# Two token blocks share each half of the first feed-forward's weights; partial sums of x1 go through DRAM

## Chip, core and metric

The kernel runs on one core of a Trainium2 chip. The metric is device time in microseconds, median over runs; lower is better. The engines are TensorE (PE; its weight loads are PEld), VectorE (DVE), ScalarE (ACT), GpSimd (POOL) and SyncE (SP, which here only issues DMAs). Each works through its own list of instructions in order, and waits where a semaphore isn't there yet.

## The reference

Chunked attention, and then two feed-forwards over its 3072 tokens of width 512. What matters of it:

```python
# attention per 32-query chunk c: keys and values = 8 memory rows + window of 56 around the chunk
scores = scale * np.matmul(q_c, k_full.transpose(0, 1, 3, 2))
a = np.exp(scores - np.max(scores, axis=-1, keepdims=True))
a = a / (np.sum(a, axis=-1, keepdims=True) + 1e-09)
out[:, :, c_start:c_end] = np.matmul(a, v_full)
...
h = x @ w_in                                              # 512 -> 2048
g = np.where(h > 0.0, h, np.exp(np.minimum(h, 0.0)) - 1)  # ELU
x1 = g @ w_out                                            # 2048 -> 512
...
y = ((x1 @ w1) * (x1 @ w2)) @ w3 @ w_out2
```

The inputs of the feed-forwards are 64-bit floats in DRAM.

## The kernel before

The tokens are cut into NB = 8 blocks of TB = 384, and a block into GPB = 3 attention groups of 128 queries (24 groups G in all). Every product is made of three passes in a 32-bit format (`mm3`, L125 to L128): each operand is split in a high part (cast on ACT) and a low part (subtraction on DVE).

**First feed-forward.** FF1 = 16 tiles of 128 columns. Iteration n = 16j + f works on block j and tile f. Below, H(n) is `mm_h` (12 matmuls into one of two PSUM banks), E(n) the ELU (`elu_exp`: two ACT steps; `elu_split`: L472 on DVE, a cast on ACT, L123 on DVE) and X(n) is `mm_x` (12 matmuls that add to PSUM banks 0 to 3). PE has them in the order H(n), X(n-2), H(n+1), X(n-1), and so on. After a block's last X, `store_x1` copies banks 0 to 3 out (two copies on ACT, two on DVE) and stores them in DRAM (`x1d`). At such a boundary X stands ahead of H in the first two iterations of the next block.

**The feed.** `Feed` turns the 32 weight tiles of this feed-forward (w_in: slots 0 to 15, w_out: slots 16 to 31) from 64-bit rows into high and low parts. Job i is spread over three steps: `rebase` on ACT (L161) once the raw tile has landed, then `shift` and `low` on DVE (L165, L169), then the cast `hi_of` on ACT (L174) and `lo_of` on DVE (L177). 34 steps finish 32 jobs. A step also loads a raw tile some jobs ahead, 512 KB on SP's queue. The intermediate `f` lies in the pool f_p, four buffers, which the copies of `store_x1` (name `st`) share.

**Attention.** A group goes through `at_turn` (T: transposes of q and k, three copies on ACT), `at_turn2` (U: four small transposes, two copies), `at_scores` (S), `at_max`, `at_sum`, `at_norm`, `at_flip` (DVE, with one exponential on ACT), `at_values` (V) and `at_out` (a cast on ACT, L123 on DVE, into xhl, the input of the first feed-forward). From group 3 on they all use one PSUM pair ("banks") and one buffer of each tile, and the next group's q, k and v are loaded as soon as those are free. Groups 0 to 2 run ahead of the first iteration by the list START, in which "f" is a feed step and "t0 u0 s0 m0 z0 n0 p0 v0 o0" are group 0's parts. The other groups are spread over the iterations by `plan`: parts at steps 0 to 9 from a group's start, two steps in an iteration, 32 steps for three groups. From group 6 on the steps also carry the conversion of the second feed-forward's weights (`mid_jobs`).

**Second feed-forward.** In the last block of the first, freed weight slots are refilled and `load_x1`/`split_x1` bring x1 of block 0 back into xhl; then w3 and w_out2 are multiplied together, and the eight blocks run through `mm_ab` and `mm_o`.

Of the kernel before, what the change touches and what calls it, by code (L numbers as in the profile page):

```python
# [19 lines left out]
def tile_kernel(  # L20
# [41 lines left out]
    AT_BLOCK = 32  # L62
# [5 lines left out]
    LATER = (10, 11, 12, 13, 14, 15, 25, 26, 27, 28, 29, 30, 31)  # L68
# [25 lines left out]
    wabd = [[dram.tile([P, 2, 512], F32, name=f"wabd{c}_{r}") for r in range(2)] for c in range(FF2)]  # L94
    x1d = [dram.tile([P, KT, TB], F32, name=f"x1d{j}") for j in range(NB)]
# [93 lines left out]
    class Feed:  # L189
# [222 lines left out]
    def store_next():  # L412
# [14 lines left out]
    for G in range(GPB, NG):  # L427
        s0 = AT_BLOCK * (G - GPB) // GPB
        for at, fn in plan:
            steps[s0 + at].append((fn, G))  # L430
        if G >= GM:
            n = [(G - GM + i) * n_others // (NG - GM) for i in range(2)]
            for job, at in zip([others.pop(0) for _ in range(n[1] - n[0])], (0, 6)):
                mid_jobs.append(job)
                for i, fn in enumerate((rebase, mid_low, mid_split)):
                    steps[s0 + at + i].append((fn, job))
                if at == 0 and w3s:
                    job = w3s.pop(0)
                    mid_jobs.append(job)
                    for at3, fn in ((4, rebase), (5, mid_low), (9, mid_flip)):  # L440
                        steps[s0 + at3].append((fn, job))
    assert not others and not w3s
    at_done, at_most = [0], [0]

    def at_step():
        if at_done[0] < min(at_most[0], len(steps)):
            store_next()
            for fn, G in steps[at_done[0]]:
                fn(G)
            at_done[0] += 1  # L450
# [3 lines left out]

    def mm_h(n):
        j, f = divmod(n, FF1)
# [19 lines left out]
    def mm_x(n):  # L476
        j, f = divmod(n, FF1)
        g, w = g_t.pop(n), W[FF1 + f]
        for o in range(KT):
            c = slice(o * P, (o + 1) * P)  # L480
            mm3(PS[o][:, 0:TB], w[:, 0, c], w[:, 1, c], g[:, 0, :], g[:, 1, :], f == 0, f == FF1 - 1)

    def store_x1(j):
        for o in range(KT):
            t = f_p.tile([P, 512], F32, tag="f", name="st")
            copy_on("av"[o % 2], t[:, 0:TB], PS[o][:, 0:TB])
            nc.sync.dma_start(out=x1d[j][:, o, :], in_=t[:, 0:TB])
# [69 lines left out]
    with tc.manual_schedule():  # L557
# [12 lines left out]
        def run(what):  # L570
            for ch in what:
                if ch == "f":
                    feed.step()
                else:
                    at_step()
# [30 lines left out]
        for n in range(NH + 2):  # L606
            j, f = divmod(n, FF1)
            while f == 0 and at_done[0] < min(AT_BLOCK * j, len(steps)):
                at_step()
            at_most[0] = AT_BLOCK * (j + 1)  # L610
            first = f < 2 and j > 0
# [6 lines left out]
            if n == FF1:  # L618
# [6 lines left out]
            if n >= 2 and first:  # L625
                mm_x(n - 2)
                if f == 1 and n < NH:
                    store_x1(j - 1)
# [100 lines left out]
```

## Time and profile before

| | |
|---|---|
| median of 3 runs | 1152.84 us (1149.68 to 1154.06) |
| the profiled execution's own time | 1151.45 us |
| its span, first to last instruction | 1149.7 us |
| PE busy | 1095.1 us, 95% of the span, 8800 matmuls |
| DVE busy, ACT busy | 493.9 us (43%), 431.2 us (38%) |
| DMA | 124.78 MB, mean 109 GB/s |

Shares over the whole span hide that the kernel has stages. In the 40 slices of the page PE reads 3, 6 and four times 8 tenths before it comes to 9, and DVE reads 4, 5 and four times 8 in the same slices and 5 and 6 afterwards. So the start and block 0, up to about 145 us, are to be read apart from the rest: there the rows below ask who is busy and who waits, engine by engine, in order of time.

### The profile page before, as it was taken

What the parts mean: (1) busy time and instruction counts of PE and PEld (TensorE: products, weight loads), DVE (VectorE), ACT (ScalarE), POOL (GpSimd) and SP (SyncE); (2) the same over time, 40 slices, a digit from 0 to 9 for tenths busy, and PEclk for the clock granted to TensorE, in tenths of its full rate; (3) what the DMA queues carried; (4) which work ended last, traced back from release to release, by engine and by line L of the source; (5) the groups of instructions that cost most, each with busy time, mean ns of one, the idle gap of its engine ahead of it and who ended that gap; (6) DMA issues with size and microseconds to landing.
All of it is one profiled execution on the core that took longest, in us unless ns stands there. A gap on an engine that the chain in (4) does not pass through costs nothing.

```text
span 1149.7 us, 20882 instructions
## 1 busy us (share of the span) xinstructions
PE 1095.1 (95%) x8800; PEld 1031.9 (90%) x8800; DVE 493.9 (43%) x912; ACT 431.2 (38%) x897; POOL 2.1 (0%) x16
## 2 busy tenths in 40 slices
PE   3688899999999999999999999999999999999998
PEld 2587789989989999999999998799999999999997
DVE  4588855555655565565655331122221212222111
ACT  3366545454544555444544441122221212122111
POOL 0000000000000000000000000000000000000000
PEclk8699999999999999999999999999999999999999
DMA  8855454444554533643630885310000101000000
GB/s 182 230 143 152 123 169 133 146 148 118 153 152 128 167 118 109 175 129 110 180 101 38 271 280 176 112 32 28 28 29 28 55 1 56 29 28 28 1 28 28
DMA packets 153100, 124.78 MB, mean 109 GB/s; under 512 B 103856, under 2 KB 136624, under 8 KB 153008
## 3 DMA queue, kind: packets, MB, share of 16 engines
q1 hardware_dynamic: 151968, 123.20, 36.0%
q8 instruction: 69, 1.13, 0.4%
q10 hardware_dynamic: 1040, 0.26, 0.1%
q14 instruction: 23, 0.19, 0.1%
HBM read 89.88 MB, written 33.55 MB: 107 GB/s over the span
## 4 chain that ended last, share of the span: by engine, by line
PE 83%; DVE 7%; ACT 4%; DMA 3%; issue 1%; SPq 1%; DVEq 0%; ACTq 0%
PE bank L126 22%; PE bank L128 21%; PE bank L127 21%; PE banks L126 4%; PE banks L128 4%; PE banks L127 4%; PE banks L378 2%; DMA x1d<-st 1%; PE banks L319 1%; DVE f L169 1%; DVE w L177 1%; ACT g L122 1%; DMA vw<-in_v_dram 1%; DVE eg L472 1%; PE banks L293 1%
## 5 line engine op out<-in xcount | busy, mean ns | idle before, releaser
L126 PE MATMUL bank<-xhl,w 128*128 128x384 f32 x768 | 266.9, 347 | 11.7 <-DVE eg L472 9.1
L128 PE MATMUL bank<-xhl,w 128*128 128x384 f32 x768 | 260.7, 339 | 0.0
L127 PE MATMUL bank<-xhl,w 128*128 128x384 f32 x768 | 260.3, 339 | 0.0
L122 ACT CAST g<-eg 128x384 fp32r<-128x384 f32 x192 | 98.4, 512 | 297.0 <-DVE eg L472 156.5
L126 PE MATMUL bank<-g,w 128*128 128x384 f32 x512 | 176.8, 345 | 0.0
L128 PE MATMUL bank<-g,w 128*128 128x384 f32 x512 | 172.3, 337 | 0.0
L127 PE MATMUL bank<-g,w 128*128 128x384 f32 x512 | 172.1, 336 | 0.0
L123 DVE TENSOR_TENSOR g<-eg,g 128x384 fp32r<-128x384 f32 x192 | 107.3, 559 | 133.9 <-ACT g L122 133.9
L126 PEld LDWEIGHTS bank<-xhl,w 128*128 128x128 f32 x768 | 146.4, 191 | 20.0 <-DVE eg L472 8.0
L538 DVE TENSOR_TENSOR eg<-eg,banks 128x384 f32<-128x384 f32 x64 | 35.4, 553 | 271.8 <-PE banks L128 271.8
L127 PEld LDWEIGHTS bank<-xhl,w 128*128 128x128 f32 x768 | 146.4, 191 | 3.2 <-DVE xhl L123 0.4
L128 PEld LDWEIGHTS bank<-xhl,w 128*128 128x128 f32 x768 | 146.1, 190 | 0.0
L126 PEld LDWEIGHTS bank<-g,w 128*128 128x128 f32 x512 | 96.5, 188 | 2.3
L127 PEld LDWEIGHTS bank<-g,w 128*128 128x128 f32 x512 | 96.6, 189 | 0.2 <-DVE g L123 0.2
L128 PEld LDWEIGHTS bank<-g,w 128*128 128x128 f32 x512 | 96.5, 188 | 0.0
L537 ACT COPY eg<-bank 128x384 f32<-128x384 f32 x64 | 30.7, 480 | 171.4 <-PE bank L128 171.4
L465 ACT ACTIVATE eg<-bank 128x384 f32<-128x384 f32 x128 | 62.6, 489 | 69.4 <-PE bank L128 69.4
L472 DVE SCALAR_TENSOR_TENSOR eg<-eg,bank 128x384 f32<-128x384 f32 x128 | 69.6, 544 | 41.3 <-ACT eg L466 40.9
L128 PE MATMUL banks<-xhl,w 128*128 128x384 f32 x256 | 85.7, 335 | 0.0
L126 PE MATMUL banks<-xhl,w 128*128 128x384 f32 x256 | 85.6, 335 | 0.0
L127 PE MATMUL banks<-xhl,w 128*128 128x384 f32 x256 | 85.6, 334 | 0.0
L128 PE MATMUL bank<-w,g 128*128 128x512 f32 x192 | 76.0, 396 | 0.0
(99 smaller groups left out, 1290.6 us busy)
## 6 DMA issues: line engine op xcount, KB each, us to landing
raw<-in_moe_w_dram SPq DMA_DIRECT2D x32, 512.0 KB
raw<-in_moe_w_out_dram SPq DMA_DIRECT2D x20, 512.0 KB
w3d<-st SPq DMA_DIRECT2D x16, 512.0 KB
wabd<-st SPq DMA_DIRECT2D x16, 512.0 KB
w<-w3d SPq DMA_DIRECT2D x16, 512.0 KB
w<-wabd SPq DMA_DIRECT2D x16, 512.0 KB
raw<-in_moe_w_in_dram SPq DMA_DIRECT2D x12, 512.0 KB
x1d<-st SPq DMA_DIRECT2D x32, 192.0 KB
```

The costliest lines, as they stand in the source:

```text
L122: nc.scalar.copy(hi, src)
L123: nc.vector.tensor_tensor(out=lo, in0=src, in1=hi.bitcast(F32), op=ALU.subtract)
L126: mm(o, lhsT=w_hi, rhs=x_hi, start=start, stop=False)
L127: mm(o, lhsT=w_hi, rhs=x_lo, start=False, stop=False)
L128: mm(o, lhsT=w_lo, rhs=x_hi, start=False, stop=stop)
L169: nc.vector.scalar_tensor_tensor(out=t, in0=l, scalar=29, in1=t, op0=ALU.logical_shift_right, op1=ALU.bitwise_or)
L177: nc.vector.tensor_tensor(out=job.to[:, 1, :], in0=job.f if src is None else src, in1=job.to[:, 0, :].bitcast(F32), op=ALU.subtract)
L378: mm(o, lhsT=vw[cc, u, 2 * hp + r, :], rhs=pT[cc, r, hp, u, :], start=u == 0, stop=u == 1)
L465: nc.scalar.activation(e, h_t[n], AF.Relu, scale=-1.0)
L472: nc.vector.scalar_tensor_tensor(out=e, in0=e, scalar=-1.0, in1=ph, op0=ALU.add, op1=ALU.max)
L537: nc.scalar.copy(e, pab[0])
L538: nc.vector.tensor_tensor(out=e, in0=e, in1=pab[1], op=ALU.mult)
```

## The change

Blocks 0 and 1 now go through tiles 0 to 7 one after the other, and then both through tiles 8 to 15 (`PARTS`); blocks 2 to 7 stay as they were. `seq` gives the block and tile of iteration n, so n = 0 to 7 is block 0, 8 to 15 block 1, 16 to 23 block 0 again, 24 to 31 block 1 again. At the end of each half the sums are stored: the first halves into `x1p`, the second into `x1d`, so that there are boundaries at n = 8 and n = 24 beside those at 16 and 32. For blocks 0 and 1 `load_x1` loads both, and `split_x1` adds them on DVE (four additions a block). The feed's jobs are in the order of the halves; its two steps an iteration go on up to n = 17, and begin at n = 0 instead of n = 2. Block 1's attention (groups 3 to 5) has to be done by n = 8 and runs at the pace "fast", half as many steps from part to part; block 2's begins at step 38 rather than 32. START has one feed step less, and v0 stands ahead of u2 and s2.

```diff
-    START = "t0 u0 f s0 t1 f m0 u1 s1 z0 n0 m1 p0 f t2 u2 s2 v0 z1 n1 p1 o0 m2 v1 f z2 n2 p2 o1 v2 f o2 f"
-    IN_BLOCK0 = ("fa", "fa", "")
+    START = "t0 u0 f s0 t1 f m0 u1 s1 z0 n0 m1 p0 t2 v0 u2 s2 f z1 n1 p1 o0 m2 v1 f z2 n2 p2 o1 v2 f o2"
+    HALF = FF1 // 2
+    PARTS = [(0, 0, HALF), (1, 0, HALF), (0, HALF, FF1), (1, HALF, FF1)] + [(j, 0, FF1) for j in range(2, NB)]
...
+    x1p = [dram.tile([P, KT, TB], F32, name=f"x1p{j}") for j in range(2)]
...
+    paces = {
+        "slow": (0, 1, 1, 2, 3, 4, 5, 6, 8, 8, 9), "fast": (0, 0.5, 0.5, 1, 1.5, 2, 2.5, 3, 4, 4, 4.5),
+        "mid": (0, 1, 1, 2, 3, 4, 5, 5, 7, 7, 7.5),
+    }
...
+    def base(G):
+        if G < 2 * GPB:
+            return 5 * (G - GPB), "fast"
+        if G < 3 * GPB:
+            return ((38, "slow"), (47, "mid"), (55, "mid"))[G - 2 * GPB]
+        return 4 * FF1 + 2 * FF1 * (G - 3 * GPB) // GPB, "slow"
...
+    seq = [(j, f, f - f0, f == f1 - 1) for j, f0, f1 in PARTS for f in range(f0, f1)]
...
-    def store_x1(j):
+    def store_x1(j, to):
...
+            for src in ((x1d, x1p) if j < 2 else (x1d,)):
+                t = late.tile([P, TB], F32, tag="x1" if src is x1d else "x1p", name="x1", bufs=4)
...
+            if len(ts) > 1:
+                nc.vector.tensor_tensor(out=ts[0], in0=ts[0], in1=ts[1], op=ALU.add)
...
-        order = sorted(range(2 * FF1), key=lambda i: i if i < FF1 else i - FF1 + 2)
+        order = sorted(range(2 * FF1), key=lambda i: (i % FF1 // HALF, i if i < FF1 else i - FF1 + 2))
...
+            def x():
+                if n >= 2:
+                    if n < 3 * FF1 // 2 + 2:
+                        feed.until(due[FF1 + seq[n - 2][1]])
+                    mm_x(n - 2)
+                    if at == 1 and n < NH:
+                        p = n // HALF - 1
+                        store_x1(seq[n - 2][0], x1p if p < 2 else x1d)
+                if n < FF1 + 2:
+                    feed.step()
+                at_step()
```

What the change moves on the engines, at three places. In these listings L291, L293, L305, L319 and L378 of before are L294, L296, L308, L322 and L381 of after, and L117, L161, L174, L465 and L466 are L120, L164, L177, L484 and L485.

PE, ahead of block 0, before: group 2 (its PSUM is pair_101) and the V of groups 0 and 1 (banks, pair_100).

```order
L291 MATMUL pair_101<-ident,qn 128x128 x4
L293 MATMUL pair_101<-ident,kn 128x128 x4
L305 MATMUL pair_101<-ident,kn 128x32 x4
L319 MATMUL pair_101<-kT,qT 32x64 x32
L378 MATMUL banks<-pT,vw 64x64 x32
L378 MATMUL pair_100<-pT,vw 64x64 x32
```

The same place after:

```order
L294 MATMUL pair_101<-ident,qn 128x128 x4
L296 MATMUL pair_101<-ident,kn 128x128 x4
L381 MATMUL banks<-pT,vw 64x64 x32
L308 MATMUL pair_101<-ident,kn 128x32 x4
L322 MATMUL pair_101<-kT,qT 32x64 x32
L381 MATMUL pair_100<-pT,vw 64x64 x32
```

V of group 0 has moved ahead of U and S of group 2.

PE at the first iterations, before, with buffer numbers (w0, w1, w2 are the tiles of H(0), H(1), H(2); w16 that of X(0)) and group 3's parts between them:

```order
L128 MATMUL bank4_95<-xhl0_73,w0_75 128x384
L291 MATMUL banks_94<-ident_72,qn_590 128x128 x4
L293 MATMUL banks_94<-ident_72,kn_166 128x128 x4
L126 MATMUL bank5_96<-xhl0_73,w1_76 128x384
...
L305 MATMUL banks_94<-ident_72,kn_166 128x32 x4
L126 MATMUL bank4_95<-xhl0_73,w2_77 128x384
...
L319 MATMUL banks_94<-kT_640,qT_638 32x64 x32
L126 MATMUL bank0_603<-g_643,w16_85 128x384
```

The same place after:

```order
L131 MATMUL bank4_95<-xhl0_73,w0_75 128x384
L294 MATMUL banks_94<-ident_72,qn_584 128x128 x4
L296 MATMUL banks_94<-ident_72,kn_168 128x128 x4
L308 MATMUL banks_94<-ident_72,kn_168 128x32 x4
L322 MATMUL banks_94<-kT_634,qT_632 32x64 x32
L129 MATMUL bank5_96<-xhl0_73,w1_76 128x384
...
L129 MATMUL bank4_95<-xhl0_73,w2_77 128x384
...
L381 MATMUL banks_94<-pT_736,vw_167 64x64 x32
L129 MATMUL bank0_597<-g_692,w16_84 128x384
```

T, U and S of group 3 now stand together ahead of H(1), and its V ahead of X(0).

ACT at the first boundary of before (n = 17), with the counters that each instruction waits for (DMAHW is a DMA's landing; the others name engines):

```order
L122 CAST g_1699<-eg_1682 128x384 [waits DVE_49]
L117 COPY st_1715<-bank0_603 128x384 [waits PE_49]
L117 COPY st_1721<-bank2_605 128x384 [waits PE_49]
L174 CAST st_1760<-f_1668 128x512
L465 ACTIVATE eg_1775<-bank5_96 128x384 [waits PE_49]
```

ACT at the first boundary of after (n = 9), where x1p of block 0 is stored. DMAHW6 is the landing of the store of st_1357, DMAHW0 that of st_1363, and DMAHW3 a raw tile's:

```order
L125 CAST g_1341<-eg_1330 128x384 [waits DVE_49]
L120 COPY st_1357<-bank0_597 128x384 [waits PE_49]
L120 COPY st_1363<-bank2_599 128x384 [waits DMAHW6_49,PE_49,Activation_49]
L177 CAST w25_93<-f_1314 128x512
L164 ACTIVATE f_1373<-raw_1292 128x512 [waits DMAHW3_49,DMAHW0_49,Activation_49]
L484 ACTIVATE eg_1389<-bank5_96 128x384 [waits PE_49]
```

Two feed jobs hold their `f` here, so the four copies have two buffers between them: the second copy on ACT waits for the first one's store, and the next rebase for the second one's.

## Rows read from the trace of the kernel before

**Rows 1.** Windows: busy time by engine in three stretches, with granted clock.

```profile
core 0: us, PE busy (x) PEld busy (x) DVE busy (x) ACT busy (x) POOL busy (x), PEclk, DMA share, GB/s
28.00:57.00 29.00, 18.69 (x299) 16.41 (x300) 15.67 (x28) 10.96 (x22) 0.00 (x0) 0.59 0.81 234
57.00:86.00 29.00, 25.19 (x251) 23.53 (x249) 25.15 (x47) 18.26 (x39) 0.00 (x0) 0.94 0.52 144
500.00:600.00 100.00, 100.00 (x1053) 96.00 (x1052) 58.20 (x107) 50.01 (x107) 0.00 (x0) 1.00 0.45 132
```

**Rows 2.** Timeline of DVE around two attention groups: start, us, line, [idle before].

```profile
95.68 0.69 DVE L336 TENSOR_REDUCE mx<-banks 128x8 f32<-128x512 f32 x1
...
97.01 0.55 DVE L472 SCALAR_TENSOR_TENSOR eg<-eg,bank 128x384 f32<-128x384 f32 x1
...
100.39 0.68 DVE L344 TENSOR_REDUCE sm<-e 128x8 f32<-128x512 f32 x1
...
101.64 0.42 DVE L165 TENSOR_SCALAR f<-f 128x512 int32<-128x512 int32 x1
...
103.31 1.29 DVE L356 TENSOR_TENSOR e<-e,rc 128x512 f32<-128x512 f32 x2
104.51 0.55 DVE L472 SCALAR_TENSOR_TENSOR eg<-eg,bank 128x384 f32<-128x384 f32 x1
105.64 0.56 DVE L123 TENSOR_TENSOR g<-eg,g 128x384 fp32r<-128x384 f32 x1 [0.58 <-ACT g L122]
106.12 0.42 DVE L165 TENSOR_SCALAR f<-f 128x512 int32<-128x512 int32 x1
...
107.79 1.24 DVE L367 STREAM_TRANSPOSE pT<-e 128x1024 f32<-128x1024 f32 x1
108.95 0.38 DVE L165 TENSOR_SCALAR f<-f 128x512 int32<-128x512 int32 x1
```

**Rows 3.** The same for the last steps of E(1) and E(14).

```profile
58.85 0.56 DVE L123 TENSOR_TENSOR g<-eg,g 128x384 fp32r<-128x384 f32 x1 [0.58 <-ACT g L122]
...
143.20 0.56 DVE L123 TENSOR_TENSOR g<-eg,g 128x384 fp32r<-128x384 f32 x1 [0.58 <-ACT g L122]
```

**Rows 4.** The same for group 0's output and group 2's maximum, ahead of block 0.

```profile
31.76 0.69 DVE L123 TENSOR_TENSOR xhl<-banks,xhl 128x512 fp32r<-128x512 f32 x1 [4.96 <-ACT xhl L122]
...
33.70 0.42 DVE L165 TENSOR_SCALAR f<-f 128x512 int32<-128x512 int32 x1
```

**Rows 5.** Chain of work that ended last: start, us, what; ahead of block 0.

```profile
20.76 4.07 DMA raw<-in_moe_w_in_dram
...
45.37 5.44 DMA kn<-in_k_dram
```

**Rows 6.** Timeline of PE: the first matmul of H(0), T(3), the first of H(1).

```profile
42.54 0.69 PE L126 MATMUL bank<-xhl,w 128*128 128x384 f32 x1 [0.68 <-ACT xhl L122]
...
49.53 1.12 PE L291 MATMUL banks<-ident,qn 128*128 128x128 f32 x4 [2.37 <-DMA qn<-in_q_dram]
...
51.62 0.67 PE L126 MATMUL bank<-xhl,w 128*128 128x384 f32 x1
```

**Rows 7.** Chain again: the stores at the boundaries n = 17 and n = 33.

```profile
154.51 2.76 DMA x1d<-st
...
234.37 4.45 DMA x1d<-st
```

**Rows 8.** Timeline of DVE: the second copy of `store_x1` at n = 17.

```profile
157.39 0.56 DVE L119 COPY st<-bank 128x384 f32<-128x384 f32 x1 [2.23 <-DMA x1d<-st]
```

**Rows 9.** Timeline of PE: S(6), X(16) first and last, the first matmul of H(20).

```profile
153.19 0.86 PE L319 MATMUL banks<-kT,qT 64*32 64x64 f32 x64 [1.56 <-ACT kT L308]
...
158.27 0.33 PE L126 MATMUL bank<-g,w 128*128 128x384 f32 x1
...
160.17 0.34 PE L128 MATMUL bank<-g,w 128*128 128x384 f32 x1
...
165.92 0.45 PE L126 MATMUL bank<-xhl,w 128*128 128x384 f32 x1 [0.86 <-DVE eg L472]
```

More of the change, by code (lines that the diff above doesn't have):

```diff
@@ L427, in tile_kernel @@
     for G in range(GPB, NG):
-        s0 = AT_BLOCK * (G - GPB) // GPB
-        for at, fn in plan:
-            steps[s0 + at].append((fn, G))
+        s0, pace = base(G)
+        for at, fn in zip(paces[pace], chain):
+            put(s0 + at, fn, G)
         if G >= GM:
             n = [(G - GM + i) * n_others // (NG - GM) for i in range(2)]
-            for job, at in zip([others.pop(0) for _ in range(n[1] - n[0])], (0, 6)):
+            for job, at in zip([others.pop(0) for _ in range(n[1] - n[0])], (0, 5)):
                 mid_jobs.append(job)
                 for i, fn in enumerate((rebase, mid_low, mid_split)):
-                    steps[s0 + at + i].append((fn, job))
-                if at == 0 and w3s:
+                    put(s0 + at + i, fn, job)
+                if at == 0 and w3s and pace == "slow":
                     job = w3s.pop(0)
                     mid_jobs.append(job)
-                    for at3, fn in ((4, rebase), (5, mid_low), (9, mid_flip)):
-                        steps[s0 + at3].append((fn, job))
+                    for at3, fn in ((3, rebase), (4, mid_low), (9, mid_flip)):
+                        put(s0 + at3, fn, job)
     assert not others and not w3s
-    at_done, at_most = [0], [0]
+    slot_at = [0]
     def at_step():
[L446 to L450, printed above, removed]
+        store_next()
+        for _, _, fn, arg in sorted(slots.pop(slot_at[0], ()), key=lambda x: x[:2]):
+            fn(arg)
+        slot_at[0] += 1
     h_t, eg_t, g_t = {}, {}, {}
+    seq = [(j, f, f - f0, f == f1 - 1) for j, f0, f1 in PARTS for f in range(f0, f1)]
     def mm_h(n):
-        j, f = divmod(n, FF1)
+        j, f = seq[n][:2]
         ph, w, x = PS[4 + n % 2][:, 0:TB], W[f], xhl[j % 2]
@@ L567, in tile_kernel @@
             jobs.append(weight(i))
+        first_late = min(due[i] for i in LATER)
         feed = Feed(jobs)
[L570 to L575, printed above, removed]
         load_qk(0)
@@ L606, in tile_kernel @@
         for n in range(NH + 2):
[L607 to L611, printed above, removed]
+            j, f, at, last = seq[n] if n < NH else (NB, n - NH, n - NH, False)
+            first = at < 2 and n >= 2
             if j == NB - 1 and f == 0:
@@ L624, in tile_kernel @@
                 mid_load(2)
[L625 to L628, printed above, removed]
+            def x():
[8 more added lines that the diff above has]
+                    feed.step()
                 at_step()
+            if first:
+                x()
             if n < NH:
                 if j == 0:
[L632 to L635 removed]
+                    feed.until(due[f])
                 mm_h(n)
                 elu_exp(n)
[L638 to L647 removed]
+                if n < FF1 + 2:
+                    feed.step()
+                at_step()
+            if not first:
+                x()
             if n < NH:
                 elu_split(n)
[L650 to L651 removed]
             if n >= NH - FF1:
```

52 lines of the change are left out of this document (18 added, 34 removed).

## Prediction

> **What bounds the kernel now.** I first read the busy time by stretches [rows 1]. From 500 to 600 us PE is busy all the time and DVE 58%: PE is the bound there, and in every block from 1 on. In block 0 (57 to 86 us stands for three such stretches up to 143) DVE is busy 25.15 of 29 us, and the clock is nearly full; at the start, 28 to 57 us, the clock is 0.59 and nobody is at the limit.
>
> So I next read DVE's timeline in block 0, by the distance from one start to the next [rows 2]. One feed job takes 1.67 us of DVE (106.12 to 107.79: shift, low and lo_of). One E takes 1.61 (104.51 to 106.12), 0.58 of it idle, for the cast on ACT between its two steps. A group's attention takes 1.33 (maximum, 95.68 to 97.01), 1.25 (sum, 100.39 to 101.64), 1.20 (norm, 103.31 to 104.51), 1.16 (transpose, 107.79 to 108.95) and 0.6 for the output, 5.55 in all. An iteration of block 0 has two jobs, one E and 3/16 of a group: 4.95 + 1.04 = 6.0 us. PE needs 12 matmuls at 0.173 us for an H or an X (158.27 to 160.17 is 11 of them [rows 9]), 2.08 each, 4.16 an iteration and some 0.7 for attention. So PE waits for DVE in block 0, and what the change is worth is first a question of what it takes off DVE there.
>
> From the end of E(1), 59.3, to that of E(14), 143.7, pass 84.4 us [rows 3]. DVE's work in it: 13 E (20.9), 25 times shift and low (1.07, 26.7), 26 times lo_of (0.60, 15.6), three groups less one output (16.05): 79.3. So 5.1 us of it is waiting.
>
> **The change, part by part.** The point that decides: the feed still takes two steps an iteration and is only ordered by halves. With 5 steps in START and two an iteration its 34 steps are done at n = 14; before, with 6 in START and one in n = 0 and 1, at n = 15. The weights of tiles 8 to 15 aren't needed before n = 16 now, but DVE converts them in n = 8 to 14 all the same. Groups 3 to 5 must be done by n = 8 instead of n = 16. So DVE has the same work in the first fifteen iterations as before, only more of it early: about 7.2 us an iteration up to n = 7, then 4.95. Both are above PE's 4.16. Block 0's gap between DVE and PE, some 17 us in all, is therefore not won; what is left are waits.
>
> (1) START. Before, DVE idles 4.96 us ahead of group 0's output [rows 4]: V(0) stands behind S(2), this behind ACT's copies, and these behind a rebase that waits for a raw tile to land at 24.8 [rows 5]. Now V(0) is ahead of U(2), and the rebase behind S(2). What is late next: ACT casts w0's high part only after U(2)'s copies. I put DVE's lo_of(0) at 24.0 (estimate: just ahead of that landing, which U(2) waits for no longer). Then 0.6 + 1.25 + 1.20 + 1.16 + 0.6 + 1.33 = 6.1 us bring group 2's maximum to an end at 30.2, before 33.7 [rows 4]: 3.5 us gained. Bounds: 2.1 if DVE starts behind the landing and its rebase, 25.4; 4.96 if the whole wait goes. H(0) then starts at 39.0 instead of 42.54 [rows 6], still at half clock, and ends at 43.6.
>
> (2) Group 3's loads and its T, U, S. On SP's queue q and k now stand behind one raw load less, whose wait for DVE was some 3 us: k is issued at 45.37 - 3.5 - 3.0 = 38.9 and lands after 5.44 at 44.3 [rows 5]. PE's wait of 2.37 ahead of T(3) shrinks to under 1. But U and S stand between T(3) and H(1): T ends at 45.4, ACT's copies 1.56 (taken from the wait in [rows 9]), U 0.6, copies 0.5, S 1.2 at half clock, so H(1) starts at 49.2 against 51.62. E(1) waits for it: H(1) 4.5, two ACT steps 1.0 and a cast 0.5, then on DVE lo_of 0.6, sum 1.25, norm 1.2, a job 1.67, transpose 1.16, E 1.61: 62.7, against 59.3. By then DVE is a job (1.67) and four parts of group 3 (4.94) ahead, 6.6. (1) and (2) together: 3.3 us gained.
>
> (3) The fast pace, E(1) to E(14). Work as before less the 6.6. Waits: V(3) follows its transpose in the next step, and DVE waits some 0.8 for the output. T(4) may begin only then (one PSUM pair). T 0.9, copies 1.5, U 0.4, H(3) 2.1, two ACT steps 1.0 and a cast 0.5 make 6.4 us until DVE can do its next lo_of; it has a job, an E and a shift and low, 4.3, in between: 2.1 idle. For group 5, H(5) stands ahead of T(5): 1.1 idle. In all 4.0 against 5.1: 1.1 gained. Bounds: none of these waits (5 gained) and both groups like group 4 with ACT's queue full (2 lost).
>
> (4) The new boundary at n = 8, 9. DVE is the bound there, so its two copies count, 2 x 0.5 = 1.0. Two feed jobs hold two of the four `f` buffers. So copy three and four wait for the landing of stores one and two, and the next rebase, on ACT in front of E(9), for the landing of store three: two landings in a row, 5.5 by the 2.76 of the boundary at n = 17 [rows 7], with copies between; DVE covers 1.67 of it with a job that is ready. That leaves 4.2 idle. Together 5.2 lost. With the 4.45 of n = 33 it is 8.6. I take 2.76, since that store also had one or two raw loads just ahead of it. The Trainium skill speaks against such a round trip: DMA: Bandwidth & Descriptors, section "Anatomy of one DMA", gives each DMA a fixed 2.0 us, mostly for the confirmation of the last write, and a fit of 2.0 us plus bytes over 436 GB/s, for DMAs issued from GpSimd. For 196,608 bytes that is an estimate of 2.45; by it this term would be 4.6, and the sum 0.6 lower. The measured 2.76 and 4.45 stand above it.
>
> (5) The boundary at n = 16, 17 has no feed, no attention and no second-layer job beside it any more (group 6 starts at n = 19). Before, from the end of E(14) at 143.7 to H(20) at 165.92 [rows 3, 9] PE had eight H or X (16.6) and T, U and S of group 6 (1.9): 3.7 of 22.2 are waits, for ACT's kT behind a rebase (1.56) and for E (0.86), among others; DVE's wait for a store [rows 8] is behind the latter. After, four free buffers take the copies, X(16) has H(17) and H(18) ahead of it, and I see no wait but small gaps: 3.1 gained.
>
> (6) The new boundary at n = 24, 25, beside groups 6 and 7, where DVE has slack: like others in full blocks, a wait of PE for E at 0.86 [rows 9] and a smaller one: 1.2 lost (0 to 2).
>
> (7) The additions: four times 0.5 on DVE each for blocks 0 and 1, in series with four casts: E(n+1) comes 4.5 us later once, while H(n+2) has 4 us and more of PE work ahead of it. 0.2 lost, up to 1. Without that cover it would be 4.5 twice. The stores and loads of x1p, 3.1 MB, fall where the DMAs are half idle or nobody waits for them.
>
> Sum: -3.3 - 1.1 + 5.2 - 3.1 + 1.2 + 0.2 = -0.9. From the profiled execution's 1151.45 that is 1150.6; from the median, 1152.84, it is 1151.9. I say 1151.5: no change that a measurement of this kernel can tell, which takes about 0.5%, 6 us.
>
> **The rivals.** *Faster, the waits go too.* START's whole 4.96 us, two thirds of the waits that (3) leaves (2.5 of 4.0), and only one landing at n = 9 because copies one and two are out early (2.8 less): -0.9 - 1.5 - 2.5 - 2.8 = -7.7, 1144. For it: DVE's waits before come from PE having T and U in different steps, and are gone. Against: ACT's order at n = 9 has both landings in one queue.
>
> *Slower, the partial sum's round trip.* At n = 8 two 512 KB raw loads are issued just ahead of the stores, and such a load takes 4.07 to land by itself [rows 5]. If stores land behind them after 4.45 to 5.9 us, two in a row cost 3.4 to 6.3 more: 1154 to 1157; with START at its lower bound, 1.4 more, 1159. The result is slower by more than 0.5% from a landing of about 6 us on.
>
> *The change does more than I see: PE alone bounds n = 0 to 15.* Then most of the 17 us would go, 1139. It would need a feed that is stretched over n = 16 and beyond; the steps of the feed speak against it.
>
> **How the numbers follow.** No change that can be told 0.51; faster 0.28 (0.26 the waits, 0.02 PE alone); slower 0.21. The range from 1142 to 1160 reaches a little over the ends of the first two rivals and should hold the time 8 times in 10; the forecast's own range is 1146 to 1157.
>
> **What would show it.** Right: DVE busy some 90% up to about 95 us and over 80% up to 145; H(0) at 39; E(14) ends within 3 us of 145; at n = 9 a copy on ACT and the rebase behind it each wait for the landing of a store of x1p; no PE wait at n = 17. Wrong: E(14) done by 138 or so (the waits of (3) and (4) are not there), or a landing at n = 9 above 5 us, or a loss of several us at the additions or in the last block.

## The result, and the profile after

| | before | after |
|---|---|---|
| median | 1153.45 us (1149.68 to 1154.87, 4 runs) | 1166.1 us (1165.6 to 1166.25, 4 runs) |
| ratio | 1 | 1.0114 (1.0089 to 1.0139) |
| the profiled execution, and its span | 1151.45, 1149.7 us | 1165.6, 1163.8 us |

The change makes the kernel 1.1% slower. The prediction, 1151.5 us with a range from 1142 to 1160, was wrong. The profiled executions differ by 14.15 us, the medians by 12.65.

The page of after: span, busy times, and the 40 slices of PE, DVE and the granted clock.

```profile
span 1163.8 us, 20920 instructions
...
PE 1101.9 (95%) x8800; PEld 1038.8 (89%) x8800; DVE 500.8 (43%) x924; ACT 432.0 (37%) x901; POOL 2.1 (0%) x16
...
PE   4667899999999999999999999999999999999998
...
DVE  4677745655655655565655341032212212122221
...
PEclk7677999999999999999999999999999999999999
```

PE reads 6, 7 and 8 where before's page reads 8, and DVE 7, 7 and 7 where it reads 8: the loss lies in block 0's stretch, and nobody is busier there. The windows of [rows 1], of after, with two more of the same length:

```profile
core 0: us, PE busy (x) PEld busy (x) DVE busy (x) ACT busy (x) POOL busy (x), PEclk, DMA share, GB/s
28.00:57.00 29.00, 18.38 (x240) 16.41 (x240) 19.18 (x33) 12.32 (x26) 0.00 (x0) 0.60 0.95 260
57.00:86.00 29.00, 18.56 (x200) 17.22 (x200) 20.52 (x40) 13.26 (x29) 0.00 (x0) 0.81 0.35 93
86.00:115.00 29.00, 20.97 (x272) 19.76 (x273) 21.09 (x39) 15.12 (x31) 0.00 (x0) 0.79 0.42 112
115.00:143.00 28.00, 24.85 (x132) 24.50 (x131) 20.75 (x39) 16.57 (x34) 0.00 (x0) 0.92 0.73 218
500.00:600.00 100.00, 98.71 (x1044) 94.00 (x1043) 57.85 (x105) 49.50 (x106) 0.00 (x0) 1.00 0.48 142
```

From 57 to 86 us DVE was busy 25.15 us of 29 at a clock of 0.94 [rows 1]; now it is 20.52, at 0.81, and PE has fallen from 25.19 to 18.56. Both wait. The timeline of PE shows for what (start, us, instruction, [idle before, and what ended it]):

```profile
62.10 2.01 PE L381 MATMUL banks<-pT,vw 64*64 64x64 f32 x64 [5.50 <-DVE pT L370]
...
87.36 2.01 PE L381 MATMUL banks<-pT,vw 64*64 64x64 f32 x64 [5.22 <-DVE pT L370]
...
110.47 2.03 PE L381 MATMUL banks<-pT,vw 64*64 64x64 f32 x64 [4.08 <-DVE pT L370]
```

These are V of groups 3, 4 and 5: each waits 4 to 5.5 us for DVE's transpose, 14.8 us in all. Before, PE waited 2.8 us ahead of V in block 0, at groups 4 and 5:

```profile
109.08 1.28 PE L378 MATMUL banks<-pT,vw 64*64 64x64 f32 x64 [1.59 <-DVE pT L367]
...
142.24 1.28 PE L378 MATMUL banks<-pT,vw 64*64 64x64 f32 x64 [1.24 <-DVE pT L367]
```

In after, PE runs at half its clock, 1.2 GHz, behind each of its three waits; the windows that begin with them:

```profile
62.00:68.00 6.00, 5.89 (x76) 5.73 (x77) 5.07 (x11) 4.10 (x8) 0.00 (x0) 0.50 0.53 148
87.00:93.00 6.00, 5.64 (x78) 5.49 (x79) 4.24 (x9) 1.10 (x3) 0.00 (x0) 0.57 0.38 80
110.00:116.00 6.00, 5.53 (x75) 5.42 (x76) 5.06 (x10) 4.12 (x8) 0.00 (x0) 0.50 0.48 156
```

And the wait comes back to DVE. DVE's timeline behind group 3's transpose:

```profile
60.81 1.24 DVE L370 STREAM_TRANSPOSE pT<-e 128x1024 f32<-128x1024 f32 x1
...
67.85 0.55 DVE L491 SCALAR_TENSOR_TENSOR eg<-eg,bank 128x384 f32<-128x384 f32 x1
71.98 0.56 DVE L126 TENSOR_TENSOR g<-eg,g 128x384 fp32r<-128x384 f32 x1 [3.58 <-ACT g L125]
...
76.33 0.69 DVE L180 TENSOR_TENSOR w<-f,w 128x512 fp32r<-128x512 f32 x1 [2.73 <-ACT w L177]
```

and ACT's in the same stretch:

```profile
69.23 0.58 ACT L298 COPY qT<-banks 128x512 f32<-128x512 f32 x1 [2.58 <-PE banks L296]
...
71.42 0.53 ACT L125 CAST g<-eg 128x384 fp32r<-128x384 f32 x1
74.74 0.49 ACT L484 ACTIVATE eg<-bank 128x384 f32<-128x384 f32 x1 [2.79 <-PE bank L131]
...
75.69 0.60 ACT L177 CAST w<-f 128x512 fp32r<-128x512 f32 x1
```

and PE's first transpose of T(4):

```profile
68.05 0.71 PE L294 MATMUL banks<-ident,qn 128*128 128x128 f32 x4
```

This is to be read as one ring. V(3) waits for DVE, which is busy meanwhile. X(0) behind it takes 4.0 us at half clock, so T(4) starts at 68.05. The first of ACT's copies of T(4) waits 2.58 us for it, and E(2)'s cast, whose input DVE had ready at 68.40, stands behind five such copies: it runs at 71.42, and DVE has waited 3.58 us. Then ACT's first step of E(3) waits for H(3), most of it at half clock; a weight's cast stands behind that, and DVE waits 2.73 us more. So DVE is late with group 4 too, and V(4) waits 5.22 us.

**Where the 14.15 us come from**, by the starts of E(n)'s first DVE step (an iteration's own clock):

| start of | E(1) | E(7) | E(9) | E(14) | E(32) | E(112) | E(127) |
|---|---|---|---|---|---|---|---|
| before | 57.72 | 97.01 | 110.57 | 142.11 | 232.86 | 634.19 | 694.51 |
| after | 61.97 | 116.22 | 131.46 | 154.39 | 243.55 | 648.14 | 708.64 |
| later by | 4.25 | 19.21 | 20.89 | 12.28 | 10.69 | 13.95 | 14.13 |

Some of the 19 us at E(7) are work that comes earlier; 8.6 come back between E(9) and E(14). DVE's idle time in the whole stretch from E(1) to E(14) is 13.5 us before and 25.7 after (stretch less busy time): 12.2 us more, of which 9.6 lie between E(1) and E(7) and 3.9 between E(7) and E(9); from E(9) to E(14) there are 1.3 less.

### The profile page after: what moved, and what is told of

It is laid out like the page before. It is cut to its first block, busy times and chain, and to the rows that moved or that the text cites. A ratio compares the mean times of both kernels' runs of the same rounds, so it can differ in the third digit from the quotient of the medians.

```text
span 1163.8 us, 20920 instructions
## 1 busy us (share of the span) xinstructions
PE 1101.9 (95%) x8800; PEld 1038.8 (89%) x8800; DVE 500.8 (43%) x924; ACT 432.0 (37%) x901; POOL 2.1 (0%) x16
## 4 chain that ended last, share of the span: by engine, by line
PE 84%; DVE 7%; ACT 3%; DMA 2%; issue 2%; SPq 1%; DVEq 0%; ACTq 0%
PE bank L129 22%; PE bank L131 21%; PE bank L130 21%; PE banks L129 4%; PE banks L130 4%; PE banks L131 4%; PE banks L381 2%; PE banks L322 1%; DMA x1d<-st 1%; DVE e L359 1%; DVE w L180 1%; DVE f L172 1%; PE banks L294 1%; PE banks L296 1%; DVE eg L491 1%
## 5 line engine op out<-in xcount | busy, mean ns | idle before, releaser
L484 ACT ACTIVATE eg<-bank 128x384 f32<-128x384 f32 x128 | 62.6, 489 | 67.0 <-PE bank L131 67.0
```

The source lines that it names most:

```text
L484: nc.scalar.activation(e, h_t[n], AF.Relu, scale=-1.0)
```

## The experiments

The table has the starts of E(n) in each profile, and the medians; ratios are to runs of the kernel before on the same chip. The E(n) are of one profiled execution each, whose own time is 1165.01 us in e7_fast, 1151.39 in e12_fill and 1159.18 in e10_spread, 3 to 5 us from their medians.

| kernel | E(1) | E(7) | E(9) | E(14) | E(32) | median | ratio |
|---|---|---|---|---|---|---|---|
| after + busy PE (e1_fill) | 63.10 | 113.72 | 128.63 | 151.56 | 240.68 | 1158.21 | 1.005 (1.0027 to 1.0072) |
| after, earlier transpose (e2_flip) | 63.56 | 113.86 | 129.32 | 152.24 | 241.41 | 1161.34 | 1.0071 (1.0053 to 1.0089) |
| after, own store buffers (e3_store) | 62.47 | 116.54 | 128.94 | 151.92 | 241.03 | 1161.05 | 1.0067 (1.0049 to 1.0084) |
| before + START alone (e4_start) | 50.34 | 89.41 | 102.97 | 135.54 | 228.21 | 1147.95 | 0.995 (0.9932 to 0.9968) |
| before + fast pace alone (e7_fast) | 61.79 | 119.69 | 130.85 | 154.64 | 242.48 | 1162.02 | 1.0056 (1.0035 to 1.0078) |
| before + V one step nearer (e5_near) | 57.52 | 96.82 | 110.42 | 141.18 | 235.72 | 1154.44 | 0.999 (0.9976 to 1.0004) |
| after + stretched feed (e8_thin) | 60.99 | 116.04 | 129.60 | 148.85 | 240.10 | 1160.37 | 1.0047 (1.0027 to 1.0067) |
| after + old offsets (e6_mid) | 62.73 | 118.40 | 133.72 | 156.64 | 245.75 | 1164.52 | 1.0082 (1.006 to 1.0104) |
| after + four edits (e9_all) | 61.60 | 113.75 | 122.89 | 141.44 | 232.05 | 1152.35 | 0.998 (0.9968 to 0.9991) |
| after, looser pace (e10_spread) | 63.33 | 114.08 | 129.38 | 152.31 | 241.41 | 1164.42 | 1.008 (1.0055 to 1.0104) |
| before + START, V later (e11_vlate) | 50.43 | 88.18 | 101.74 | 134.11 | 225.38 | 1146.29 | 0.9933 (0.9913 to 0.9953) |
| before + START + busy PE (e12_fill) | 53.41 | 92.66 | 106.22 | 138.83 | 232.24 | 1147.57 | 0.9947 (0.993 to 0.9964) |

The theory from the profile of after was: group by group, block 1's attention is one chain through PE, ACT and DVE with one PSUM pair; at the fast pace each of its waits is paid (**queues**), and the low clock behind the waits doubles what PE does next (**clock**). Its rivals: the round trip of the x1p stores, START, and the order in halves itself.

**Is it the concentrated attention, or the halves?** The kernel before, with only the fast pace of groups 3 to 5:

```diff
+        pace = [at for at, _ in plan]
+        if G < 2 * GPB:
+            s0, pace = 5 * (G - GPB), (0, 0, 0, 1, 1, 2, 2, 3, 4, 4, 4)
-        for at, fn in plan:
+        for at, (_, fn) in zip(pace, plan):
```

> The kernel before (its own START, whole blocks, its own feed), with one thing of the change: groups 3 to 5 run at the fast pace, ten half steps... that is, parts at steps 0, 0, 0, 1, 1, 2, 2, 3, 4, 4, 4 from a group's start and a group every 5 steps, so that they are done by n = 9. No half blocks, no x1p. Theory A, the concentrated attention itself is the loss (waits ahead of V at a low clock, and T, U and S in one step behind ACT's queue): E(7) starts 12 to 18 us later than in the kernel before (8 of it is the 1.5 groups' DVE work that comes earlier), of which about 8 come back by n = 14, so E(14) is 5 to 9 us later and the whole 1158 to 1163 us; PE waits of 2 us and more ahead of V(3), V(4), V(5), with the granted clock under 0.8 behind each. Theory B, the loss comes from the halves (the order of the feed, the store and its round trip at n = 8 and 9): then E(14) is within 3 us of the kernel before and the whole within 4 us of it, 1150 to 1158.

PE's waits ahead of V in this kernel's timeline, and the windows behind two of them:

```profile
70.71 2.01 PE L378 MATMUL banks<-pT,vw 64*64 64x64 f32 x64 [5.09 <-DVE pT L367]
...
94.06 2.01 PE L378 MATMUL banks<-pT,vw 64*64 64x64 f32 x64 [5.42 <-DVE pT L367]
...
119.82 2.01 PE L378 MATMUL banks<-pT,vw 64*64 64x64 f32 x64 [3.83 <-DVE pT L367]
```

```profile
70.00:76.00 6.00, 5.29 (x75) 5.17 (x76) 5.07 (x10) 4.09 (x8) 0.00 (x0) 0.53 0.36 78
94.00:100.00 6.00, 5.93 (x78) 5.78 (x79) 4.24 (x9) 1.10 (x3) 0.00 (x0) 0.54 0.43 89
```

The same three waits and the same clock, in whole blocks and with no x1p. E(14) starts at 154.64, 12.5 us later than in the kernel before; DVE's idle time from E(1) to E(7) is 16.9 us, against 16.2 in after and 6.6 in before. Theory A holds and was even too mild (5 to 9 us later was expected). The concentrated attention by itself is enough for a loss as large as after's in block 0. That E(14) is within 0.3 us of after's is chance: E(7) is 3.5 us later here, and E(7) to E(9), where after has its new boundary, 4.1 us shorter. In the whole this kernel lost 0.56%, inside the expectation, and half of after's 1.14%.

**What the low clock costs of it.** In after, 24 needless 128x384 matmuls ahead of each of the three V, into the PSUM bank that V then fills; they keep PE at work while it would wait:

```diff
+        if GPB <= G < 2 * GPB:
+            for _ in range(24):
+                mm(PA[:, 0, 0:TB], lhsT=W[0][:, 0, 0:P], rhs=xhl[0][:, 0, 0, :], start=True, stop=True)
```

> The changed kernel with 24 matmuls (128x384, into the attention's PSUM pair, which V overwrites) put on PE just ahead of V of groups 3, 4 and 5, where PE waited 5.5, 5.2 and 4.1 us; they add work and compute nothing that is used. Theory 'clock': the loss of the first eight iterations comes from the granted clock falling to 1.2 GHz in these waits (0.50, 0.57 and 0.50 in the windows behind them), so that V, X, T and H behind each take twice as long. Then clock stays over 0.95 from 57 us on, V takes 1.1 instead of 2.0, X 2.2 instead of 4.0, and the kernel is 6 to 9 us faster than the changed one, 1157 to 1160. Rival 'queues': in-order waits on one PSUM pair at any clock; then no gain, 1164 to 1168.

The windows that stand above for after, at the same times:

```profile
62.00:68.00 6.00, 4.12 (x81) 3.73 (x82) 5.07 (x10) 4.08 (x8) 0.00 (x0) 1.00 0.63 166
87.00:93.00 6.00, 3.40 (x25) 3.09 (x24) 4.37 (x8) 4.23 (x10) 0.00 (x0) 1.00 0.67 171
110.00:116.00 6.00, 6.00 (x36) 6.00 (x36) 5.08 (x10) 4.21 (x9) 0.00 (x0) 1.00 0.71 165
```

The full clock is granted in all of them. E(14) comes 2.83 us earlier, DVE idles 12.7 instead of 16.2 us from E(1) to E(7). So the clock is about 3.5 of the 9.6 us lost there; the rest is waiting at full clock. The median came out as "clock" expected, but block 0 gave only 2.8 us of that: in the profile another 4.5 us come behind E(32), in code that this run shares with after, where other runs differ as much (see e6_mid).

**What the distance of V costs.** In after the transpose stands a step earlier among the parts (`"fast"`: 2.7 instead of 3):

```diff
-        "fast": (0, 0.5, 0.5, 1, 1.5, 2, 2.5, 3, 4, 4, 4.5),
+        "fast": (0, 0.5, 0.5, 1, 1.5, 2, 2.5, 2.7, 4, 4, 4.5),
```

> The changed kernel with the transpose (at_flip) of the fast pace one step earlier, in the same step as the norm, so that V of groups 3 to 5 stands two steps behind it instead of one. Theory 'clock' and rival 'queues' both expect shorter waits of PE ahead of V (3 to 4 us instead of 4 to 5.5) and a gain of 2 to 5 us: 1161 to 1164. If the loss came from the new boundary at n = 8, 9 (rival 'round trip'), nothing changes: 1165 to 1167.

V's waits shrink from 14.8 to 8.8 us (3.92, 2.28 and 2.57), and the windows behind them show a higher clock than after's 0.50, 0.57 and 0.50:

```profile
62.00:68.00 6.00, 5.15 (x77) 4.71 (x77) 5.05 (x11) 3.83 (x8) 0.00 (x0) 0.72 0.68 161
83.00:89.00 6.00, 5.59 (x83) 5.15 (x75) 5.01 (x10) 4.42 (x9) 0.00 (x0) 0.72 0.51 114
```

E(14) comes 2.15 us earlier. Six microseconds less waiting on PE gave two: ACT's queue ahead of U (waits of PE of 4.7 us there, 4.1 before the edit) is the next link of the same ring.

**The other way about: T, U and S apart.**

```diff
-        "fast": (0, 0.5, 0.5, 1, 1.5, 2, 2.5, 3, 4, 4, 4.5),
+        "fast": (0, 1, 1, 1.5, 2, 2.5, 3, 3.5, 4, 4, 4.5),
```

> The kernel after with the fast pace loosened: T at step 0, U and S at 1, maximum and sum at 1.5 and 2, norm 2.5, transpose 3 and the loads between, V still at 4. U no longer stands directly behind T, so an H or X covers ACT's copies. Theory queues, that the packing of T, U and S in one step costs several us: PE's waits ahead of U (1.47 and 2.59) go, DVE's idle time between E(1) and E(7), about 12 us, falls by 3 or more, E(7) comes at 113 or earlier, whole 1161 to 1163. Theory distance, that what counts is how far V stands behind the transpose: the transpose now ends later, V's waits of 5.5, 5.2 and 4.1 grow by 1 to 3 each, the granted clock stays under 0.6 behind them, and E(7) is at 116 to 122, whole 1165 to 1171.

Both theories are half right, so this run doesn't decide. PE's waits ahead of U fall to 0.5 us (3.1 us stand ahead of S now) and DVE's idle time from E(1) to E(7) falls by 3.6, as "queues" said; but V's waits add up to 16.3 us, the first being

```profile
63.46 2.01 PE L381 MATMUL banks<-pT,vw 64*64 64x64 f32 x64 [7.79 <-DVE pT L370]
```

and the median, 1164.42, is not to be told from after's. At this pace what one link gives, another takes.

**Is a wait ahead of V always a loss?** The kernel before at its own pace, with the transpose one step nearer to V:

```diff
+            if fn is at_flip and G < 2 * GPB:
+                at = 7
```

> The kernel before, with one step of distance less between the transpose and V of groups 3 to 5 (the transpose a step later), at the old pace and in whole blocks. If the wait of PE ahead of V comes from that distance alone, PE waits 1 to 3 us ahead of each V, the granted clock falls under 0.8 behind them, E(14) is 2 to 5 us late and the whole 1 to 4 us longer, 1155 to 1158. If it needs the packed pace (DVE behind by a group's other parts), the waits stay under 1 us and the whole is within 1.5 us of the kernel before.

```profile
77.51 1.28 PE L378 MATMUL banks<-pT,vw 64*64 64x64 f32 x64 [1.74 <-DVE pT L367]
...
110.55 2.01 PE L378 MATMUL banks<-pT,vw 64*64 64x64 f32 x64 [3.25 <-DVE pT L367]
...
144.07 2.00 PE L378 MATMUL banks<-pT,vw 64*64 64x64 f32 x64 [2.87 <-DVE pT L367]
```

The waits came, as the first theory said, with V at half clock in two of the three; the median did not change, as the second said. At the old pace DVE has work of its own while PE waits (its idle time from E(1) to E(7) is 6.6 us as before). So the wait of 3.25 us ahead of V(4), with the low clock behind it, cost nothing, since it didn't come back to DVE within the same chain: E(14) starts 0.9 us earlier than before. The third wait is not free in this profile. Behind V(5) the feed is at its end, E(14) to E(15) takes 6.19 us instead of 3.12, and E(32) is 2.9 us late; the medians don't show that loss, and why is open.

**What the round trip costs.** In after, block 0's four x1p copies lie in two buffers of the pool of `g`, instead of the pool of the feed's `f`:

```diff
+            if to is x1p and j == 0:
+                if o % 2 == 0:
+                    pair_t = g_p.tile([P, 2, TB], F32R, tag="g", name="g")
+                t = pair_t[:, o % 2, :].bitcast(F32)
+            else:
+                t = f_p.tile([P, 512], F32, tag="f", name="st")[:, 0:TB]
```

> The changed kernel with block 0's first partial sums copied into two buffers of the ELU's output (three of them, one in use) instead of the feed's pool, so that no copy and no rebase waits for a store's landing at n = 9. Rival 'round trip': the stores are what costs; 6 us or more faster, under 1160. Theory 'clock': the interval from E(8) to E(9) falls from 8.6 to some 6 us, of which the rest of the feed keeps most; 1 to 3 us faster, 1163 to 1165.

In after the boundary at n = 9 stands in the chain of waits and in the timelines of ACT and DVE like this:

```profile
124.32 1.87 DMA x1p<-st
```

```profile
126.29 0.48 ACT L120 COPY st<-bank 128x384 f32<-128x384 f32 x1 [2.00 <-DMA x1p<-st]
126.99 0.56 DVE L122 COPY st<-bank 128x384 f32<-128x384 f32 x1 [2.01 <-DMA x1p<-st]
...
128.71 0.67 ACT L164 ACTIVATE f<-raw 128x512 f32<-128x512 f32 x1 [1.41 <-issue]
```

ACT's copy waits 2.00 us for the first landing, and the rebase another 1.41 us, as the prediction said (the profile names no releaser for it; by its counters it waits for the landing of the second store). With the new buffers both waits are gone, E(8) to E(9) takes 5.86 us instead of 8.64, and E(14) comes 2.47 us earlier. The round trip is a part of the loss, and not its main part.

**What the crowded feed costs.** In after, from n = 8 on one feed step an iteration, and a second at n = 9, 12 and 15:

```diff
-                if n < FF1 + 2:
+                if n < HALF or n in (9, 12, 15):
                     feed.step()
```

> The kernel after, with the feed stretched: from n = 8 on one step an iteration and three more (n = 9, 12, 15), so that its 34 steps end at n = 17 instead of 14; the second halves' weights are still converted ahead of their use. The prediction's third rival rested on such a feed. If DVE bounds n = 8 to 14, as the prediction said, E(9) to E(14), 22.9 us in the kernel after, takes 20.8 to 21.5, E(14) comes 1.5 to 2.5 us earlier plus 1.7 for a job less at the boundary n = 8 and 9, and the whole is 1162 to 1164. If PE or the round trip of the stores bounds there, E(14) moves under 1 us and the whole is 1165 to 1167.

E(9) to E(14) takes 19.25 us instead of 22.93, and E(14) comes 5.54 us earlier, more than expected. DVE did bound the iterations from E(9) to E(13), as the prediction said: each of the four takes 4.93 or 4.94 us in after, the 4.95 that the prediction worked out for two jobs and an E, and taking jobs away there gives time back at once.

**START alone.** The kernel before with only the new START:

```diff
-    START = "t0 u0 f s0 t1 f m0 u1 s1 z0 n0 m1 p0 f t2 u2 s2 v0 z1 n1 p1 o0 m2 v1 f z2 n2 p2 o1 v2 f o2 f"
+    START = "t0 u0 f s0 t1 f m0 u1 s1 z0 n0 m1 p0 t2 v0 u2 s2 f z1 n1 p1 o0 m2 v1 f z2 n2 p2 o1 v2 f o2"
```

> The kernel before with the changed kernel's START list alone (V of group 0 ahead of U and S of group 2, one feed step less). By the prediction H(0) starts at 39 to 40 instead of 42.5 and 2 to 4 us are won: 1149 to 1151. If the start hides nothing on the path (DVE takes the feed step later), no change: 1152 to 1154.

It is 0.5% faster than the kernel before. Its PE at H(0), T(3) and H(1), and the window behind them:

```profile
39.72 0.69 PE L126 MATMUL bank<-xhl,w 128*128 128x384 f32 x1 [0.68 <-ACT xhl L122]
...
44.13 0.72 PE L291 MATMUL banks<-ident,qn 128*128 128x128 f32 x4
...
45.04 0.42 PE L126 MATMUL bank<-xhl,w 128*128 128x384 f32 x1
```

```profile
50.00:56.00 6.00, 5.99 (x94) 5.58 (x94) 5.32 (x11) 4.08 (x10) 0.00 (x0) 1.00 0.95 226
```

H(0) starts 2.8 us earlier than in [rows 6], T(3) without the wait of 2.37, and H(1) at 45.04 instead of 51.62 and at full clock (PE had the clock at 0.59 from 50 to 56 us in the kernel before). So the 2.8 us have become 7.4 by E(1), and 6.1 in the medians. How much of the rest is the wait that T(3) no longer has and how much the clock isn't told apart.

**The second-layer jobs.** After with their offsets as before:

```diff
-            for job, at in zip([others.pop(0) for _ in range(n[1] - n[0])], (0, 5)):
+            for job, at in zip([others.pop(0) for _ in range(n[1] - n[0])], (0, 6)):
...
-                    for at3, fn in ((3, rebase), (4, mid_low), (9, mid_flip)):
+                    for at3, fn in ((4, rebase), (5, mid_low), (9, mid_flip)):
```

> The kernel after with the second layer's jobs at the offsets of the kernel before (second job at step 6 instead of 5; the w3 job's rebase and low at 4 and 5 instead of 3 and 4). Open is the 2.8 us that the kernel after loses in blocks 2 to 7. If the offsets cause it, 1 to 3 us come back, E(122) minus E(36) as in the kernel before (2 to 3 us shorter), 1163 to 1165. If it is only where a store happens to land at a boundary, the loss moves among the boundaries and the whole is within 1 us of the kernel after.

No effect of the offsets is shown; the intervals of the two ratios overlap. The profile is 2.2 us behind after at E(14) and level with it at E(127), but what it regains it regains at one boundary, n = 65, where the pair E(64) to E(66) takes 14.27 us in after, 11.90 here and 11.94 in before. In after the store's landing shows there in the chain, and PE waits 1.29 us for E:

```profile
407.81 4.52 DMA x1d<-st
```

```profile
421.18 0.45 PE L129 MATMUL bank<-xhl,w 128*128 128x384 f32 x1 [1.29 <-DVE eg L491]
```

In before and in e1_fill the copy at this place waited 2.1 us for its store. The old offsets aren't needed for it: e1_fill, e2_flip and e8_thin keep those of after, and the pair takes 12.43, 12.08 and 12.34 us there, in e3_store 14.66. From E(32) to E(112) the seven profiles with after's code in blocks 2 to 7 take 400.1 to 404.6 us, and the six with before's 400.7 to 405.0; after's own 404.6 is at the long end. So no run shows that the change costs anything in these blocks.

**All four repairs.** After with the edits of e1_fill, e2_flip, e3_store and e8_thin together.

> The kernel after with four edits at once: 24 needless 128x384 matmuls ahead of each V of groups 3 to 5 (they only keep PE at work), the transpose a quarter step earlier in the list so that it stands one step earlier, block 0's x1p copies in buffers of their own pool, and the stretched feed. If the loss in block 0 lies in these four places and they add, E(14), 154.4 in the kernel after, comes at 142 to 145 (2.8 + 2.2 + 2.5 + 5.5 less, some of it twice counted), and the whole is 1150 to 1155, so no slower than the kernel before. If the loss is in something they share, as DVE's and ACT's order in n = 1 to 8, E(14) stays at 147 or later and the whole at 1156 to 1160.

The windows of block 0 in this kernel:

```profile
57.00:86.00 29.00, 25.27 (x307) 23.40 (x306) 21.52 (x40) 12.89 (x28) 0.00 (x0) 0.88 0.35 93
86.00:115.00 29.00, 25.78 (x262) 24.26 (x259) 21.64 (x42) 15.55 (x33) 0.00 (x0) 0.94 0.54 135
115.00:143.00 28.00, 28.00 (x163) 28.00 (x162) 23.09 (x44) 20.68 (x42) 0.00 (x0) 1.00 0.68 206
```

E(14) starts at 141.44, 12.95 us earlier than in after; the four single gains add up to 2.83 + 2.15 + 2.47 + 5.54 = 12.99. Together they are as large as the loss, 12.28 us. But that the two sums agree is chance, for stretch by stretch they don't. E(7) comes 2.50 us earlier in e1_fill alone, 2.36 in e2_flip alone, and no more than 2.47 here; from E(7) to E(9) the four win 6.1 us, and the single runs 4.6 in all. The busy PE and the earlier transpose mend the same wait, and together they do too much: DVE ends group 4's transpose at 82.81, and PE is at the 24 matmuls until V(4).

```profile
80.62 4.32 PE L377 MATMUL banks<-xhl,w 128*128 128x384 f32 x24
84.87 1.16 PE L384 MATMUL banks<-pT,vw 64*64 64x64 f32 x64
```

In e2_flip, without them, V(4) started at 82.75. Fewer of them might give more; no run shows it. And the stretched feed's part is no repair of what the change added: it is a gain that the halves allow and that the change didn't take. The whole is 1152.35 us, 0.2% below the kernel before. PE is now busy all the time from 115 to 143 us, which is what a feed in halves could give; and still it is 0.3% behind the kernel with START alone.

**Better than both.** The kernel before with START, and V and its output of groups 3 to 5 a step later:

```diff
+            if fn in (at_values, at_out) and G < 2 * GPB:
+                at = 9
```

> The kernel before with the START of the change, and V with its output of groups 3 to 5 one step later (9 instead of 8 from the group's start). The kernel with that START alone took 1147.95 and had PE waits of 1.56 and 2.01 ahead of V, with a granted clock of 0.74 and 0.72 behind them. If distance is what counts, these waits go and with them the low clock, E(14) comes 1 to 3 us earlier than its 135.5, whole 1145 to 1147.5. If DVE's load sets the pace anyway (block 0 is bound by DVE in the kernel before), E(14) is within 1 us and the whole 1147 to 1149.5.

1146.29 us, 0.7% faster than before, is the fastest kernel here. PE's wait ahead of V(4), 1.56 us in e4_start, is gone; the one ahead of V(5) is not (1.99 us, 2.01 in e4_start), and V(3) had none there:

```profile
102.23 1.16 PE L378 MATMUL banks<-pT,vw 64*64 64x64 f32 x64
```

E(14) is 1.4 us earlier than in e4_start; in the whole the intervals of the two overlap, so V's step can't be told from nothing.

**The clock in that kernel.** Instead, 10 needless matmuls ahead of V, as in e1_fill but in the kernel with START.

> The kernel before with the START of the change and 10 needless 128x384 matmuls ahead of V of groups 3 to 5, some 1.7 us at full clock, into a PSUM bank that V then fills. If the clock behind PE's waits costs something in this kernel too, the granted clock of 0.74 and 0.72 rises to 0.9 and more, E(14) comes up to 1.5 us earlier, whole 1146 to 1148. If DVE bounds there and the clock costs nothing, E(14) is the same or up to 1 us later, whole 1147.5 to 1150.

PE's wait ahead of V falls from 3.6 to 0.3 us, and the whole, 1147.57, is that of e4_start. The E(n) of its profile are 3 us late from E(1) on, but there q and k of group 3 landed later and T(3) waited 1.49 and 0.43 for them, ahead of any V. From E(1) to E(14) it takes 85.42 us, e4_start 85.20: no gain, and the medians say the same. The clock behind these waits costs nothing that can be told where DVE isn't kept waiting.

## Why the prediction was wrong, point by point

**What bounds block 0.** That DVE sets the pace of the kernel before, and that the feed's steps keep the 17 us from being won, was right: e8_thin gained 5.5 us by taking jobs off DVE. What failed is to go on from "DVE is the bound at its old pace" to "DVE stays 90% busy at the fast one". It was busy 71% from 57 to 86 us (20.52 of 29). The prediction's 7.2 us an iteration up to n = 7 (its own rows add up to 7.0) was the work alone; from E(1) to E(7) an iteration took 9.04.

**(1) and (2), START and group 3.** H(0) at 39.0 was predicted, 39.81 measured; the end of E(1) at 62.7, and it is 63.6. The sum was right to 1 us. What the step missed is that the same START in the old order is worth 6.1 us: H(1) comes 6.6 us sooner there, and PE is at its full clock some 10 us sooner (the matmuls of H follow at 0.17 us from 45 us on, before and after only from 55). In after T, U and S stand between H(0) and H(1), and that gain is gone. The kernel before was a poor measure of what START was worth, since after hides it.

**(3), the fast pace, is the step that failed.** It predicted 1.1 us gained; instead DVE idles 9.6 us more up to E(7), and 1.3 less from E(9) to E(14). E(14) ends at 156.1 us, where the prediction had some 145. It put DVE's wait for group 3's output at 0.8 us, which took 0.29, and DVE's idle time of group 4 at 2.1, which took 3.58 + 2.73 = 6.3. Four things were wrong in it. It costed V(3) from DVE's side only, one operation behind the transpose, and not from PE's: PE had finished H(2) at 56.6 and had nothing to do for 5.5 us. It let T(4) begin at group 3's output, while X(0) stands between V(3) and T(4) on PE and ran until 68.05. It took PE's times at full clock behind that (H(3) 2.1, measured 3.5); the granted clock was 0.50 from 62 to 68 us. And it let ACT's cast of E(2) come when its input is ready, while five copies of T and U stand ahead of it in ACT's list. Its lower bound, "both groups like group 4 with ACT's queue full", 2 lost, was still one passage at full clock, so the range didn't reach what happened. e1_fill puts the clock at some 3.5 us of it, and e7_fast shows that the pace by itself is enough for a loss of this size.

**(4), the round trip.** The mechanism is as predicted, with both landings waited for. E(8) to E(9) took 8.64 us against 4.93 in the iterations behind: 3.7 lost, where 5.2 was predicted. e3_store, with no wait for a landing, gives back 2.8 of it. The first landing took 1.87 us, not 2.76. By the Trainium skill (DMA: Bandwidth & Descriptors, section "Anatomy of one DMA"), whose fit gave an estimate of 2.45, the term would have been 4.6; the measured landing is below the estimate here, and 4.52 at n = 65 well above it.

**(5), n = 16, 17.** 3.1 gained was predicted. From E(14) to H(20) pass 19.71 us instead of 23.81, 4.1 less, of which 0.9 is S(6), which comes later now: 3.2. Right, and no wait of PE stands there.

**(6), n = 24, 25.** 1.2 lost was predicted; from H(20) to E(32) it is 2.5, with the 0.9 of S(6) in it: 1.6. The size was right, the place was not. PE doesn't wait at the boundary but at T(7), 1.40 us for a PSUM pair that the w3 job still holds, and at V(7), 0.96 for DVE, at the new pace "mid".

**Not in the sum:** blocks 2 to 7, E(32) to E(112), take 404.6 us instead of 401.3, 3.3 more. Most of it (2.3) is the landing at n = 65. Seven profiles with the same code there take from 400.1 to 404.6 us, so none of it need belong to the change (see e6_mid).

**(7), the additions.** 0.2 predicted, 0.2 measured (E(112) to E(127)). E(121) comes 8.55 us behind E(120), and the next iterations make it up.

**The rivals.** The slower one was the round trip, with 1154 to 1159; its mechanism is real, but smaller than the forecast's own. The loss came by a rival that the text didn't have: the concentrated chain loses on all three engines at once. The rival "PE alone bounds n = 0 to 15" was right about what it would need, a stretched feed: e8_thin and e9_all have it, and in e9_all PE is busy 28 of 28 us from 115 to 143 us (25.62 in e8_thin).

## What to carry to other kernels

When a chain that crosses engines (PE, ACT, DVE and back) is pressed into half the steps, cost it from each engine in turn: what stands behind the waiting instruction in that engine's own list, and whether that comes back to the chain. A wait that is covered (V(4) in e5_near: 3.25 us, free) and one that returns to its own chain (e7_fast: 12.5 us later at E(14)) look the same in a list of waits. And where a change has parts that don't need each other, measure them apart: here one line of it gave 0.5% and the rest cost more than 1.5%.

## What the runs showed of the hardware

Behind PE's waits of 5.50, 5.22 and 4.08 us ahead of V the windows read a granted clock of 0.50, 0.57 and 0.50, and behind 3.92 and 2.28 in e2_flip 0.72; in e1_fill, where 1.45 and 1.26 us are left of them, 1.00. The length of the wait alone doesn't decide it: behind 2.78 us in e10_spread (V(4), window 85 to 91 us) the clock is 1.00 too. Half clock means 1.2 GHz: V took 2.01 us instead of 1.16 to 1.28. The Trainium skill (TensorE: Matmul & The Clock Gate, section "Why this matters for your kernels") advises against long idle gaps between bursts of matmuls, since the clock drops; the traces agree, with these numbers. V(4) in e5_near adds that the drop costs nothing where another engine sets the pace.

A store of the same 196,608 bytes landed after 1.87 us (n = 9 of after) and 4.52 us (n = 65), and in the kernel before after 2.76 and 4.45 [rows 7]. One number for a landing was not enough even within one kernel.
